# Two lone token tiles joined into a pair, batch 0's token transform with its two sums in the other order, and its first tile centred in halves

## The chip, the core and the metric

The kernel runs on one core of a Trainium2 chip. The metric is the device time of one launch in microseconds (us). A core has five engines that run side by side, each through its own list of instructions in order: PE (TensorE, matmul, with PEld for the weight loads that run ahead of it), DVE (VectorE), ACT (ScalarE), POOL (GpSimd) and SP (SyncE, which here only issues DMAs). They wait for one another by semaphores.

## The reference

For each of 8 batches there are 12 heads, 448 tokens and 64 channels per head. What is computed, cut to what matters:

```python
q_n = q / (norm(q, axis=-1) + 1e-06);  k_n likewise
attn = softmax(q_n @ k_n.T / tau)            # per head, tau = 0.1
x = (attn @ v) as (batch, 448, 768)          # heads side by side
mixed = real(fft(fft(x, axis=1), axis=2))    # tokens, then channels
u = x + mixed
un = (u - mean(u)) / sqrt(var(u) + 1e-06)    # per token
out = u + relu(un @ w_ch1) @ w_ch2           # 768 -> 3072 -> 768
```

## The kernel before

**Tiles.** The 448 tokens of a batch are held in tiles of 128. The Fourier transform is real-valued sums and differences with tables of cosines and sines, and it leaves the tokens folded: an even batch gives three whole tiles, and half a tile that shares its place with a half of the odd batch behind it; that shared tile is the odd batch's fourth. So `tiles` (L1312) lists three tiles for an even batch and four for an odd one, 28 in all.

**Stages of a batch.** `attn` (L907) makes scores (L973, L986), exponentials on ACT (L951) and the product with v (L1004, L1010). `fold` and `fsum` (L1038, L1111) sum over tokens with the token tables (matmuls L1129, L1134, L1138; their result is copied out of PSUM at L1159/L1160). `fft` (L1165) does the channel sums: the matmuls at L1181 in batch 0 and at L1188/L1191 in the others. Each batch has two of these groups, called fd0 and fd1. `uadd` adds x (L1233, L1245), and then each tile is normalised: mean (L1270/L1271), squares on ACT (L1275), logarithm and exponential (L1278, L1280), and the centring on DVE (L1282) into the buffer UN. A tile is then turned, in batch 0 by PE (L1292, copied out at L1300), in all others by a transposing DMA that SP issues (L1303), into one of the four slots of UNT.

**The two products with the weights.** `ffn` and `up` take the tiles one at a time or in pairs. The first product (L1350) takes 144 matmuls either way: 128 columns wide for a lone tile, 256 for a pair. The second (`prod`, L1494) takes 48 matmuls of 384 columns for a lone tile. For a pair it is done in seven products of quarter matrices instead of eight, with sums of the hidden quarters made on DVE (`comb`, L1593): 84 matmuls. The last three pairs do the first product in such a way too (`ups`, L1445). `units` (L1322) sets the pairs and the slots: of an even batch two tiles are a pair and one is alone. Lone are the first tile of batches 0 and 6 and the last tile of batches 2 and 4. A pair's result leaves PSUM through ACT (L1514) with an add on POOL (L1519), or through DVE (L1530).

**What sets the order.** The program is written by a planner (`schedule`, L257). Each operation has an engine, a duration from the table `TIMES`, a priority, and what it depends on; the table `SHIFT` moves single priorities. The planner walks through time and gives each engine the operation of least priority number that can start. All products with the weights hang on one another in a chain (`self.main`), so PE does them in a fixed order, with pieces of the next batch's attention set between them. Where the plan leaves PE idle, `fill` (L398) puts in six matmuls of 128 columns that compute nothing used (L1737). Up to the first product they read the identity matrix in TX, and after it W1b.

**Batch 0's tables.** ACT makes the channel tables at L645 and L647, the second being the sine table CSp. POOL makes the negated sine table from it (L659), into the tensor CSd. In batch 0 each of fd0 and fd1 is two groups of eight matmuls, first sum 0, which reads the negated table, and then sum 1, which reads CSp.

Of the kernel before, what the change touches and what calls it, by code (L numbers as in the profile page):

```python
# [13 lines left out]
DM = H * DH  # L14
# [11 lines left out]
TF = 4  # L26
ORDER = (0, 1, 2, 3, 5, 4)
# [473 lines left out]
class Kern:  # L501
# [405 lines left out]
    def attn(self, b):  # L907
# [31 lines left out]
        for pos, j in enumerate(ORDER):  # L939
# [20 lines left out]
            elif b >= 4:  # L960
                steps = [[(pos, kt) for kt in range(3)]]
            else:
                steps = [[(pos, 0), (pos, 1)], [(pos, 2), (pos + 1, 0)]] if pos % 2 == 0 else [[(pos, 1), (pos, 2)]]
# [201 lines left out]
    def fft(self, b):  # L1165
# [94 lines left out]
        for ui, ut in enumerate(order):  # L1260
# [24 lines left out]
            if b == 0 and ui == 0:  # L1285
                self.un0 = un
# [511 lines left out]
```

## Time and profile before

| what | value |
|---|---|
| runs of the kernel, median (lowest to highest of 3) | 577.16 us (577.0 to 578.32) |
| span of the profiled execution | 575.2 us |
| PE busy | 555.8 us, 97% of the span |
| DVE, ACT, POOL busy | 430.6, 385.3, 220.3 us |
| granted TensorE clock, mean | 0.999 of full speed |

The span runs from the first to the last instruction of the profiled execution; that execution's time as a run is not recorded apart from the three runs. "Busy" is the share of time in which at least one instruction of the engine ran; matmuls overlap, so sums of single durations are longer than the busy time. A bracket at the end of a timeline row is the time that the engine stood idle just before it, and who ended the wait. In the chain of waits the time given for a run of matmuls is from start to start, without the overlap.

### The profile page before, as it was taken

What the parts mean: (1) busy time and instruction counts of PE and PEld (TensorE: products, weight loads), DVE (VectorE), ACT (ScalarE), POOL (GpSimd) and SP (SyncE); (2) the same over time, 40 slices, a digit from 0 to 9 for tenths busy, and PEclk for the clock granted to TensorE, in tenths of its full rate; (3) what the DMA queues carried; (4) which work ended last, traced back from release to release, by engine and by line L of the source; (5) the groups of instructions that cost most, each with busy time, mean ns of one, the idle gap of its engine ahead of it and who ended that gap; (6) DMA issues with size and microseconds to landing.
All of it is one profiled execution on the core that took longest, in us unless ns stands there. A gap on an engine that the chain in (4) does not pass through costs nothing.

```text
span 575.2 us, 16313 instructions
## 1 busy us (share of the span) xinstructions
PE 555.8 (97%) x6766; PEld 436.2 (76%) x6766; DVE 430.6 (75%) x917; ACT 385.3 (67%) x724; POOL 220.3 (38%) x332
## 2 busy tenths in 40 slices
PE   3899999999999999999999999999999999989997
PEld 3569787676787686878788787778778787959694
DVE  8989968996669869975669669776778579986262
ACT  7898885564876885687558875577637853747270
POOL 7534414356329544612370724523270210041303
PEclk9999999999999999999999999999999999999999
DMA  9999999975459739952595429743591210023001
GB/s 188 224 233 171 166 186 130 171 152 111 111 94 103 178 76 135 142 127 62 112 121 93 102 80 147 150 84 85 89 113 29 43 57 28 2 43 72 28 28 56
DMA packets 187898, 62.20 MB, mean 108 GB/s; under 512 B 166800, under 2 KB 185616, under 8 KB 187824
## 3 DMA queue, kind: packets, MB, share of 16 engines
q1 hardware_dynamic: 129856, 38.35, 33.7%
q0 software_dynamic: 57968, 22.81, 30.9%
q8 instruction: 53, 0.87, 0.6%
q14 instruction: 21, 0.17, 0.1%
HBM read 51.90 MB, written 11.01 MB: 109 GB/s over the span
## 4 chain that ended last, share of the span: by engine, by line
PE 60%; DVE 4%; ACT 2%; issue 0%; DVEq 0%; ACTq 0%
PE PS L1494 23%; PE PS L1350 20%; PE PS L1445 6%; PE PS L1010 4%; PE PS L973 3%; DVE U L1233 1%; PE PS L1004 1%; PE PS L986 1%; ACT E L951 1%; DVE ACG L1222 1%; ACT F L1275 1%; PE PS L1134 1%; PE PS L1191 1%; DVE SM L885 1%; DVE HQ L1593 1%
## 5 line engine op out<-in xcount | busy, mean ns | idle before, releaser
L1350 PE MATMUL PS<-UNT,W1b 128*128 128x256 bf16 (+1 forms) x1872 | 186.1, 256 | 1.2 <-DMA UNT<-F 0.6
L1350 PEld LDWEIGHTS PS<-UNT,W1b 128*128 128x128 bf16 x1872 | 155.5, 98 | 20.1 <-issue 2.7
L951 ACT ACTIVATE E<-PS 128x900 bf16<-128x900 f32 (+1 forms) x192 | 148.0, 827 | 19.1 <-PE PS L973 16.6
L1494 PE MATMUL PS<-W2b,HQ 128*128 128x384 bf16 x768 | 133.1, 326 | 0.0
L896 POOL TENSOR_TENSOR QH<-STG,SM 128x256 bf16<-128x256 f32 x126 | 82.3, 679 | 91.9 <-DVE SM L702 73.3
L1494 PEld LDWEIGHTS PS<-W2b,HQ 128*128 128x128 bf16 x768 | 73.3, 98 | 46.2 <-issue 0.7
L1519 POOL TENSOR_TENSOR OUTB<-OUTB,U 128x192 f32<-128x192 f32 x66 | 43.2, 675 | 138.5 <-ACT OUTB L1514 137.3
L1366 ACT ACTIVATE HQ<-PS 128x512 bf16<-128x512 f32 x81 | 48.2, 595 | 40.0 <-PE PS L1350 39.5
L1494 PE MATMUL PS<-TX,HQ 128*128 128x384 bf16 (+2 forms) x408 | 69.7, 321 | 1.8 <-ACT MV L1278 1.6
L883 ACT ACTIVATE QH<-STG 128x384 f32<-128x384 f32 x84 | 42.7, 520 | 25.8 <-DVE SM L885 21.3
L1494 PEld LDWEIGHTS PS<-TX,HQ 128*128 128x128 bf16 x408 | 38.4, 98 | 25.7 <-ACT MV L1278 2.0
L1593 DVE TENSOR_TENSOR HQ<-HQ 128x1536 bf16<-128x1536 bf16 (+1 forms) x69 | 49.5, 721 | 9.9 <-ACT HQ L1366 7.1
L885 DVE TENSOR_REDUCE SM<-QH 128x6 f32<-128x384 f32 x84 | 44.7, 544 | 11.3 <-ACT QH L883 11.0
L1010 PE MATMUL PS<-VB,E 128*128 128x65 bf16 x1152 | 51.4, 193 | 0.0
L1366 DVE TENSOR_SCALAR HQ<-PS 128x512 bf16<-128x512 f32 x45 | 31.0, 688 | 23.8 <-PE PS L1350 23.4
L1010 PEld LDWEIGHTS PS<-VB,E 128*128 128x128 bf16 x1152 | 47.7, 97 | 1.2
L1552 POOL DMA_INDIRECT out_dram<-OUTB,IDX x21 | 23.8, 1134 | 56.9 <-DVE OUTB L1530 51.7
L1004 PE MATMUL PS<-VZ,E 128*128 128x130 bf16 x192 | 41.6, 219 | 0.5 <-ACT E L951 0.2
L973 PE MATMUL PS<-QK 64*128 64x225 bf16 (+2 forms) x864 | 39.6, 227 | 0.1
L1233 DVE SCALAR_TENSOR_TENSOR U<-ACG,X 128x768 bf16<-128x768 f32 (+4 forms) x39 | 39.1, 1015 | 0.8
L1530 DVE TENSOR_TENSOR OUTB<-PS,OUTB 128x384 f32<-128x384 f32 x33 | 18.2, 553 | 25.7 <-PE PS L1494 21.9
L1514 ACT ACTIVATE OUTB<-PS 128x384 f32<-128x384 f32 x33 | 16.1, 488 | 29.5 <-PE PS L1494 29.1
(191 smaller groups left out, 793.6 us busy)
## 6 DMA issues: line engine op xcount, KB each, us to landing
STG<-in_q_dram SPq DMA_DIRECT2D x18, 384.0 KB, 4.0
STG<-in_k_dram SPq DMA_DIRECT2D x18, 384.0 KB, 3.8
VB<-in_v_dram POOLq DMA_DIRECT2D x24, 192.0 KB, 7.1
W1b<-in_moe_w_ch_dram POOLq DMA_DIRECT2D x12, 384.0 KB, 7.7
W2b<-in_moe_w_ch_dram POOLq DMA_DIRECT2D x12, 384.0 KB, 7.2
out_dram<-OUTB SPq DMA_DIRECT2D x7, 384.0 KB, 3.4
W2b<-in_q_dram SPq DMA_DIRECT2D x2, 576.0 KB, 10.0
W2b<-in_k_dram SPq DMA_DIRECT2D x2, 576.0 KB, 10.7
```

The source lines that it names most:

```text
L885: P.add("dve", lambda v, o=SS[:, i, H // ns * x:H // ns * (x + 1)], sq=sq: v.tensor_reduce(o, sq.rearrange("p (h d) -> p h d", d=DH), AX.X ...
L896: r = v.tensor_tensor(v3(qh)[:, h:h + 4], v3(buf)[:, h:h + 4], RN[:, i, h:h + 4].unsqueeze(2).to_broadcast((128, 4, DH)), AluOp.mult)
L951: return a.activation(o, self.PS[:, bk:bk + nc_, 0:SQ2], ACTF.Exp, scale=1.0 / self.tau)
L973: i = pe.matmul(self.PS[:, bk + h, c0:c0 + n], self.KT[r, jj, kt * 128:(kt + 1) * 128], self.QT[r, jj, cols], start=True, stop=True)
L1004: r = pe.matmul(o, st(6), self.VZ[:, j, :], start=not split, stop=(split and i == 0), skip_group_check=True)
L1010: r = pe.matmul(o[:, 65 * h:65 * h + 65], st(2 * kt + h), self.VB[:, kt, 2 * j + h, :], start=(split and i == h == kt == 0), stop=((not sp ...
L1233: self.snu.append(P.add("dve", lambda v: v.scalar_tensor_tensor(two(U[o0:o0 + n, ut, :]), src, 1.0, two(X[i0:i0 + n, x, :]), AluOp.mult, A ...
L1350: r = pe.matmul(self.PS[:, bk, x * n:(x + 1) * n], self.W1b[:, j, ft * 128:(ft + 1) * 128], self.UNT[:, j, cs], start=(j == 0), stop=(j == ...
L1366: return e.activation(o, i, ACTF.Relu) if e is self.nc.scalar else e.tensor_relu(o, i)
L1494: r = pe.matmul(self.PS[:, bk, 0:n], lhs(f), rhs(f), start=(start and f == 0), stop=(stop and f == NF // 2 - 1), skip_group_check=True)
L1519: r = g.tensor_tensor(self.OUTB[:, ob, xs], self.OUTB[:, ob, xs], self.U[:, ut, xs], AluOp.add)
L1593: P.add("dve", lambda v: v.tensor_tensor(cs(o), cs(a), cs(bq), op), 0.16 + 0.3 * len(ks), -0.5, f"{nm}{ks[0]}_{b}", reads=rd, writes=[x fo ...
```

## The change

- `units` now lists the tiles of all batches in one row and takes them in pairs, but for the two named in `ONES`. The last tile of batch 4 and the first of batch 5 are a pair, then 5's second and third, then 5's fourth with the first of batch 6. So four lone tiles become two, 16 units become 15, and two pairs cross from one batch to the next.
- `HELD`: the fourth tile of batch 5 is not centred into UN, whose place the next batch's fold needs, but later, out of U into a QH buffer, behind the first product of the pair before (`unheld`).
- In batch 0, sum 1 of fd0 and fd1 comes first and sum 0 second; the negated table is tracked under a name of its own (CSm), so that only sum 0 waits for it.
- The first tile of batch 0 is centred in two halves of 384 columns, and PE turns each half by itself.
- Batch 3 issues the scores of three token blocks as one operation, as batches 4 to 7 did; before, it issued two at a time.
- Scores of a batch are ordered behind the channel sums of the batch before it.
- The planner's margins for operations that wait on DMAs are larger in four entries of `LATE`. The loads of the start are held in a written order (`QUEUES`). `SHIFT` grows from 312 names to 1751, so that operations change places in every batch.

```diff
+ONES = ((0, 0), (2, 2))
+HELD = (5, 3)
...
+QUEUES = [("ld_q1_0 ld_k0_0 ld_q0_0 ld_t0_0 ld_q2_0 ld_t1_0 ld_k1_0 ld_t2_0 ld_k2_0 ld_q0_1 ld_t0_1 ld_k0_1 ld_k1_1 ld_t1_1 ld_q1_1"),
...
-    "te0_7": {0: -660.502}, "S20": {0: 422.8735}, "c31_6": {0: 717.6321, 3: 0.5978}, "c3r1_6": {0: 473.2237}, "c41_6": {2: 825.7525},
...
-LATE = {r"W[12]_\d+": 1.5, "tmd": 2.0, r"sq\d_\d": 1.5, r"sq[KQT]\d_1": 1.5, r"ktd\d": 2.0, r"qdup\d": 2.0, ...
+LATE = {r"sq6_[2-7]": 4.0, r"W[12]_\d+": 1.5, "tmd": 2.0, r"sq\d_\d": 2.0, r"sq[KQT]\d_1": 1.5, r"ktd\d": 3.5, r"qdup\d": 4.0, ...
...
-    (0.4, 1.9), 10, "sinp", reads=["CSp"], writes=["CSd"])
+    (0.4, 1.9), 10, "sinp", reads=["CSp"], writes=["CSm"])
...
-            elif b >= 4:
+            elif b >= 3:
                 steps = [[(pos, kt) for kt in range(3)]]
...
-            for sg in (0, 1) if b == 0 else (0,):
+            for sg in (1, 0) if b == 0 else (0,):
-                                         reads=["Tt0", "Tt1", "Tt1b", "CSd"] + (["CSp"] if b == 0 and sg else []),
+                                         reads=["Tt0", "Tt1", "Tt1b", "CSd"] + ([["CSm"], ["CSp"]][sg] if b == 0 else []),
...
+            if (b, ui) == HELD:
+                self.held = (ut, rn, lp, slot, col)
+                continue
+            halves = [slice(0, 384), slice(384, DM)] if late else [slice(0, DM)]
+            for g, c in enumerate(halves):
+                un = P.add("dve", lambda v, ...: v.tensor_scalar(self.UN[:, nb_, c], U[:, ut, c], self.MV[:, ut, 0:1], ...
...
+    def unheld(self):
+        P.add("dve", lambda v: v.tensor_scalar(self.QH[:, r, :], self.U[:, ut, 0:DM], self.MV[:, ut, 0:1], self.RS[:, ut:ut + 1], AluOp.add, AluOp.mult),
+              t_dve(DM, 4) + 0.16, lp, f"un{ui}_{b}", reads=rn + [f"MV{ut}", f"RS{ut}"], writes=qn)
+        self.last_tru = P.add("sp", lambda sy, sem: sy.dma_start_transpose(self.UNT[:, :, col:col + 128], self.QH[:, r, :]).then_inc(sem, 16),
...
-            for n in (1, 2) if b in (0, self.nb - 2) else (2, 2) if b % 2 else (2, 1):
+        order = [(b, i) for b in range(self.nb) for i in range(len(self.tiles(b)))]
+        while x < len(order):
+            n = 1 if order[x] in ONES else 2
+            for y in range(n):
+                b, i = order[x + y]
+                self.slots[b][i] = 2 * (u % 2) + y
+            self.pairs.append(order[x:x + n])
...
+        for k, unit in enumerate([u for u in self.pairs if u[-1][0] == b]):
+                    self.up(b, unit, chunks, True)
+                    if unit[1][0] == HELD[0] and unit[0][0] < b:
+                        self.unheld()
```

Three places show what the planner made of it. The first is DVE in the last part of batch 6's products, where L1465 (now L1870) adds what PE left in PSUM to an earlier result, L1593 (L1999) makes the sums of hidden quarters, and L1233 (L1617) adds x for batch 7. Before:

```order
L1593 TENSOR_TENSOR HQ<-HQ 128x512
L1465 TENSOR_TENSOR HQ<-PS,E 128x384
L1233 SCALAR_TENSOR_TENSOR U,ACG<-ACG,X 97x768
L1593 TENSOR_TENSOR HQ<-HQ 128x512
L1253 COPY ACG<-ACG 1x2
L1253 COPY U<-U 1x768
L1593 TENSOR_TENSOR HQ<-HQ 128x1536
L1270 TENSOR_SCALAR MV<-ACG 128x1
L1593 TENSOR_TENSOR HQ<-HQ 128x1536
```

And in the changed kernel:

```order
L1870 TENSOR_TENSOR HQ<-PS,E 128x384 x2
L1872 TENSOR_SCALAR HQ<-HQ 128x384
L1671 TENSOR_SCALAR F<-U,MV 128x768
L1999 TENSOR_TENSOR HQ<-HQ 128x512 x2
L1999 TENSOR_TENSOR HQ<-HQ 128x1536 x2
L1606 TENSOR_TENSOR ACG<-PS,ACG 128x388
L1617 SCALAR_TENSOR_TENSOR U,ACG<-ACG,X 97x768
```

Batch 7's add of x over 97 rows, two copies and a mean stood between the last L1465 and the second large sum; they now stand behind it, and one centring (L1671) stands in front.

The second place is PE between the channel sums fd1 of batch 2 (L1188/L1191, now L1572/L1575) and the first product of that batch's first pair (L1350, now L1755). L1494 (L1899) is the second product of the unit before, L973 and L986 (L1357, L1370) are scores of batch 3, L1004 and L1010 its products with v, whose two rows come four times, right ahead of the first product. Before, behind 24 matmuls of L1494:

```order
L1494 MATMUL PS<-W2b,HQ 128x384 x8
L973 MATMUL PS<-QK 128x225 x8
L1494 MATMUL PS<-W2b,HQ 128x384 x16
L973 MATMUL PS<-QK 128x225 x8
L1494 MATMUL PS<-TX,HQ 128x384 x4
L986 MATMUL PS<-QK,KTD 128x225 x2
L1494 MATMUL PS<-TX,HQ 128x384 x8
L1004 MATMUL PS<-VZ,E 128x130
L1010 MATMUL PS<-VB,E 128x65 x6
```

And in the changed kernel, from the last two matmuls of fd1 on:

```order
L1572 MATMUL PS<-CS,E 128x96
L1575 MATMUL PS<-CS,E 128x2x96
L1899 MATMUL PS<-TX,HQ 128x384 x20
L1899 MATMUL PS<-W2b,HQ 128x384 x24
L1899 MATMUL PS<-TX,HQ 128x384 x12
L1357 MATMUL PS<-QK 128x225 x12
L2153 MATMUL PS<-W1b 128x128 x18
L1370 MATMUL PS<-QK,KTD 128x225 x2
L1755 MATMUL PS<-UNT,W1b 128x256 x24
```

Between fd1 and the first product there stood 24 + 8 + 16 + 4 + 8 = 60 matmuls of the unit before, two groups of scores, a third of two matmuls, and 28 matmuls with v. Now there are 56 of the unit before, 12 + 2 of scores and none with v, but 18 matmuls that `fill` put in (L2153). Sixteen matmuls of the unit before have gone in between fd0 and fd1, which stood side by side.

The third place is DVE behind the channel sums of batch 5 (differences L1222, now L1606; add of x L1233, now L1617; centring L1282, now L1671), whose first tile is now the partner of batch 4's last. Before, the last ten of the rows up to its centring:

```order
L1233 SCALAR_TENSOR_TENSOR U,ACG<-ACG,X 32x768
L1366 TENSOR_SCALAR HQ<-PS 128x512
L1233 SCALAR_TENSOR_TENSOR U,MV<-ACG,X 1x768
L1270 TENSOR_SCALAR MV<-ACG 128x1
L1270 TENSOR_SCALAR MV<-MV 128x1
L885 TENSOR_REDUCE SM<-QH 128x6 x2
L1366 TENSOR_SCALAR HQ<-PS 128x512
L885 TENSOR_REDUCE SM<-QH 128x6
L1366 TENSOR_SCALAR HQ<-PS 128x512
L1282 TENSOR_SCALAR F<-U,MV 128x768
```

And in the changed kernel, all rows from the differences to the centring:

```order
L1606 TENSOR_TENSOR ACG<-PS,ACG 128x388 x2
L1617 SCALAR_TENSOR_TENSOR U,ACG<-ACG,X 128x768 x2
L1606 TENSOR_TENSOR ACG<-PS,ACG 128x388
L1654 TENSOR_SCALAR MV<-ACG 128x1
L1269 TENSOR_REDUCE SM<-QH 128x6
L1606 TENSOR_TENSOR ACG<-PS,ACG 128x388
L1617 SCALAR_TENSOR_TENSOR U,ACG<-ACG,X 97x768
L1936 TENSOR_TENSOR OUTB<-PS,OUTB 128x384
L1269 TENSOR_REDUCE SM<-QH 128x6
L1671 TENSOR_SCALAR F<-U,MV 128x768
```

The first tile is centred behind 11 DVE instructions, counted from the first difference, where 27 stood before.

## Rows read from the trace of the kernel before

**Rows 1.** The page's first part: busy time, share, instructions by engine.

```profile
PE 555.8 (97%) x6766; PEld 436.2 (76%) x6766; DVE 430.6 (75%) x917; ACT 385.3 (67%) x724; POOL 220.3 (38%) x332
```

**Rows 2.** Windows: stretch, length, busy time (instructions) of each engine, clock, DMA.

```profile
0.00:48.40 48.40, 35.94 (x518) 27.82 (x518) 43.20 (x103) 41.44 (x67) 27.32 (x58) 1.00 1.31 211
48.40:571.70 523.30, 519.87 (x6250) 408.39 (x6248) 387.09 (x814) 343.83 (x658) 192.66 (x275) 1.00 0.60 99
571.70:575.20 3.50, 0.00 (x1) 0.00 (x0) 0.29 (x1) 0.00 (x0) 0.36 (x1) 0.89 0.31 112
```

**Rows 3.** Waits of PE: who, for whom, us in total, times, longest.

```profile
PE PS L1350 <- DMA UNT<-F: 0.6, 1, 0.6
```

**Rows 4.** Chain of waits: start, us from start to start, what.

```profile
236.98 4.03 PE PS L1350 x72
...
434.29 6.55 PE PS L1350 x60
```

**Rows 5.** Timeline of PE, 100 to 119: start, us, instruction, count.

```profile
103.47 13.81 PE L1494 MATMUL PS<-W2b,HQ 128*128 128x384 bf16 x84
```

**Rows 6.** Groups by form, PE: count, then busy us, mean ns, idle before.

```profile
L1350 PE MATMUL PS<-UNT,W1b 128*128 128x128 bf16 x576 | 34.1, 219 | 0.2
```

**Rows 7.** Timeline, all engines, 40.9 to 56, a choice.

```profile
40.98 1.15 ACT L759 ACTIVATE OUTB<-W2b 128x1152 f32<-128x1152 f32 x1
...
41.17 2.17 POOL L659 TENSOR_SCALAR CS<-TX 128x770 bf16<-128x770 bf16 x1 [0.31 <-ACT TX L647]
...
42.03 1.33 ACT L1159 ACTIVATE E<-PS 128x900 bf16<-128x900 f32 x2
...
42.58 1.37 PE L1737 MATMUL PS<-TX 128*128 128x128 bf16 x18 [0.17 <-DVE SM L762]
...
43.79 0.84 PE L1181 MATMUL PS<-CS,E 128*128 128x193 bf16 x8
...
46.56 0.42 DVE L1282 TENSOR_SCALAR F<-U,MV 128x768 bf16<-128x768 bf16 x1
...
47.03 0.51 PE L1292 MATMUL PS<-TX,F 128*128 128x128 bf16 x6
...
47.85 0.55 DVE L1300 CAST UNT<-PS 128x384 bf16<-128x384 f32 x1
...
48.46 7.79 PE L1350 MATMUL PS<-UNT,W1b 128*128 128x128 bf16 x126
```

**Rows 8.** Timeline of PE from fd1 of batch 2 to its first product.

```profile
182.11 4.07 PE L1494 MATMUL PS<-TX,HQ 128*128 128x384 bf16 x24
...
187.41 0.56 PE L973 MATMUL PS<-QK 64*128 64x225 bf16 x8
...
194.85 1.38 PE L1350 MATMUL PS<-UNT,W1b 128*128 128x256 bf16 x11
```

**Rows 9.** Batch 5, fd0 to first product: PE, SP and line L1303's landings.

```profile
362.16 0.21 PE L1188 MATMUL PS<-CS,E 97*128 97x96 bf16 x1
...
379.10 5.21 SPq L1303 DMA_TRANSPOSE UNT<-F  x4
...
DMA to landing us min/median/max: 2.7/2.8/5.3
...
387.59 0.78 PE L973 MATMUL PS<-QK 64*128 64x128 bf16 x24
388.30 2.79 PE L1350 MATMUL PS<-UNT,W1b 128*128 128x256 bf16 x24
```

**Rows 10.** Timeline, all engines, 503 to 507, a choice.

```profile
503.40 1.76 POOL L1519 TENSOR_TENSOR OUTB<-OUTB,U 128x192 f32<-128x192 f32 x2 [35.16 <-ACT OUTB L1514]
503.48 1.28 DVE L1593 TENSOR_TENSOR HQ<-HQ 128x1536 bf16<-128x1536 bf16 x1
...
505.22 0.96 DVE L1593 TENSOR_TENSOR HQ<-HQ 128x1536 bf16<-128x1536 bf16 x1 [0.39 <-DVE MV L1270]
...
506.32 4.06 PE L1494 MATMUL PS<-TX,HQ 128*128 128x384 bf16 x24 [1.64 <-ACT MV L1278]
```

More of the change, by code (lines that the diff above doesn't have):

```diff
@@ L977, in attn @@
                 self.last_qk = P.add("pe", fn, 0.195 * len(st_) + 0.2, pj, f"qk{j}{st_[0][1]}_{b}", reads=rd,
-                      tiles=new, acquire=new, margin=0.3, order=([self.last_qk] if self.last_qk else []) + self.pvs[-2:-1])
+                      tiles=new, acquire=new, margin=0.3, order=([self.last_qk] if self.last_qk else []) + self.pvs[-2:-1] + (self.fd_ops[-1:] if b and pos == 0 else []))
                 for tile, (ps, kt) in zip(new, st_):
@@ L1055, in fold @@
                        t_dve(512, 2) + (0.03 if b else 0.0), pj, f"f{eo}{dj}_{b}", reads=["AC0", "AC2"],
-                       writes=[f"F{eo}{dj}"] + ([f"UN{x}" for x in range(4)] if dj == 0 and eo == 0 else []),
+                       writes=[f"F{eo}{dj}"] + ([f"UN{x}{y}" for x in range(4) for y in ("", "h")] if dj == 0 and eo == 0 else []),
                        after=[self.first_f] if dj or eo else [])
@@ L1285, in fft @@
-            if b == 0 and ui == 0:
-                self.un0 = un
+            if (b, ui) == HELD:
[3 more added lines that the diff above has]
+            for g, c in enumerate(halves):
+                un = P.add("dve", lambda v, ut=ut, nb_=nb_, late=late, c=c: v.tensor_scalar(self.UN[:, nb_, c], U[:, ut, c], self.MV[:, ut, 0:1], None if late else self.RS[:, ut:ut + 1],
+                                                                                          AluOp.add, AluOp.bypass if late else AluOp.mult),
+                      t_dve(c.stop - c.start, 4) + 0.16, lp, f"un{ui}_{b}", reads=rn + [f"MV{ut}"] + [f"RS{ut}"] * (not late), writes=[f"UN{nb_}" + "h" * g] + [f"UN{nb_}h"] * (not late))
@@ L1287, in fft @@
             if b == 0:
                 tile = Tile("G")
-                def fn(pe, tile=tile, nb_=nb_):
-                    for j in range(NJ):
-                        r = pe.matmul(self.PS[:, self.bank(tile) + j // 3, 128 * (j % 3):128 * (j % 3) + 128],
-                                      self.UN[:, nb_, 128 * j:128 * j + 128], self.ID, start=True, stop=True)
-                    return r
-                P.add("pe", fn, 0.4, lp, f"tn{ui}_{b}", reads=[f"UN{nb_}", "ID"], tiles=(tile,), acquire=tile)
+                tns = []
@@ new lines, in fft, with fn @@
+                for g in range(2) if late else (None,):
+                    def fn(pe, tile=tile, nb_=nb_, g=g):
+                        for j in range(NJ) if g is None else range(3 * g, 3 * g + 3):
+                            r = pe.matmul(self.PS[:, self.bank(tile) + j // 3, 128 * (j % 3):128 * (j % 3) + 128],
+                                          self.UN[:, nb_, 128 * j:128 * j + 128], self.ID, start=True, stop=True)
+                        return r
+                    tns.append(P.add("pe", fn, 0.2 if late else 0.4, lp, f"tn{ui}_{b}", reads=[f"UN{nb_}" + "h" * (g == 1), "ID"] + [f"UN{nb_}h"] * (g is None), tiles=(tile,), acquire=None if g else tile))
@@ L1300, in ev @@
                         return e.activation(o, i, ACTF.Copy) if e is self.nc.scalar else e.tensor_copy(o, i)
-                    self.evac(ev, 384, lp, f"eu{ui}{g}_{b}", writes=[f"uT{slot}" + "xy"[g]], after=(tile.users[0],), tiles=(tile,))
+                    self.evac(ev, 384, lp, f"eu{ui}{g}_{b}", writes=[f"uT{slot}" + "xy"[g]], after=(tns[g if late else 0],), tiles=(tile,))
                 continue
@@ L1322, in units @@
     def units(self):
[L1324 to L1330 removed]
+        self.slots = [[0] * len(self.tiles(b)) for b in range(self.nb)]
+        order = [(b, i) for b in range(self.nb) for i in range(len(self.tiles(b)))]
+        u = x = 0
+        self.pairs = []
+        while x < len(order):
[4 more added lines that the diff above has]
+            self.pairs.append(order[x:x + n])
+            u, x = u + 1, x + n
     def hid(self, q, ft0, n=1):
@@ L1520, in plus @@
                 return r
-            self.P.add("pool", plus, 1.07, -1, f"{nm}p_{b}", reads=[on] + self.unames(b, ut), writes=[on])
+            self.P.add("pool", plus, 1.07, -1, f"{nm}p_{b}", reads=[on] + self.unames(bt, ut), writes=[on])
             return op
@@ L1531, in fin @@
         on = f"OUT{ob}" + "b" * c + "z" * (c0 > 0)
-        return self.P.add("dve", fn, t_dve(c1 - c0), -1, f"{nm}_{b}", reads=([on] if src == "out" else self.unames(b, ut)) + [f"RS{ut}"] * late, writes=[on],
+        return self.P.add("dve", fn, t_dve(c1 - c0), -1, f"{nm}_{b}", reads=([on] if src == "out" else self.unames(bt, ut)) + [f"RS{ut}"] * late, writes=[on],
                           after=(op,), tiles=(tile,))
@@ L1729, in build @@
             op.prio = round(op.prio + SHIFT.get(op.name, {}).get(k, 0), 4)
+        named = {op.name: op for op in self.P.ops if op.dma is not None}
+        for q in QUEUES:
+            q = [named[n] for n in q.split()]
+            for x, y in zip(q, q[1:]):
+                y.order += (x,)
         self.est = self.P.schedule()
```

88 lines of the change are left out of this document (45 added, 43 removed), and 499 rows, old and new, of tables (SHIFT, TIMES).

## The prediction, made before the changed kernel ran

> **What bounds the kernel now.** I read the engine summary first, then windows over the launch, then PE's waits, and only then the places that the change touches. In the summary PE is busy for 97% of the span, DVE for 75% [rows 1]. The windows split this into three parts [rows 2]. Up to 48.4 us, before the first product with the weights, PE works for only 35.94 us, so there a chain through other engines sets the time. From 48.4 to 571.7 us PE is busy for 519.87 of 523.30 us, which leaves 3.43 us idle in all. The last 3.5 us have no matmul. So in the long middle part PE's own work is the path: a microsecond of matmuls that goes is a microsecond off the end, as long as no new wait takes its place, and all waits together can give back at most 3.43 us. Two waits stand out: 1.64 us in the middle of batch 6's products [rows 10], and 0.6 us on a turned tile, once [rows 3].
>
> The sum is made against the profiled span of 575.2 us. The median of the runs is 577.16 us, 1.96 us more, which lies outside the span; I add it unchanged. A measurement of this kernel can tell about 0.3% from no change, 1.7 us, so "the same" is 575.4 to 578.9.
>
> **A. Two pairs in place of four lone tiles.** In the chain a lone tile's 72 matmuls of the first product take 4.03 us and a pair's 60 take 6.55 [rows 4]; both kinds have 144, so 8.06 and 15.72 us. The second product of a pair, 84 matmuls of 384 columns, takes 13.81 us with the end of the last one, 13.65 from start to start, or 0.1625 each [rows 5]; a lone tile's 48 take 7.80. Two lone tiles cost 2 x (8.06 + 7.80) = 31.72 us, a pair 15.72 + 13.65 = 29.37: 2.35 us less. That is for each two lone tiles joined; what does the whole change join? Four lone tiles become two, but in the order (4, 2), (5, 0), ... the pairs in between only shift by one, so one pair is gained: minus 2.35 us. The other bound is the group by form, where 576 lone matmuls are busy for 34.1 us, 8.5 for each of the four tiles [rows 6]; with it the saving is 2 x (8.5 + 7.8) - 29.37 = 3.3. I take 2.35, since the chain counts from start to start, which is what PE's path adds up.
>
> The row gives 4.03 / 72 = 56 ns for a matmul of 128 columns and 6.55 / 60 = 109 for one of 256. The Trainium skill (TensorE: Matmul & The Clock Gate, Back-to-back issue gap) puts a sustained stream of loads and matmuls of 128 columns at about 81 ns each. By that a lone first product would take 11.7 us and the pair save some 7 us more. The trace disagrees with the page, whose isolated gap of about 56 ns is what the rows show, and the sum goes by the rows.
>
> The pair adds seven sums of hidden quarters and a few results on DVE, and six adds on POOL. DVE is idle for a quarter of the span [rows 1] and these lie beside 29 us of matmuls, so I put them at nothing. Without that cover each would cost its length. What speaks against it: the large sum on DVE takes 0.96 us alone and 1.28 beside POOL's add [rows 10], 0.32 more for a collision; six more adds, all on DVE's path, would cost 6 x 0.32 = 1.9 us. The Trainium skill (GPSIMD Engine Reference, Specifications) says why this may be: POOL's SBUF interfaces are shared with VectorE, and an instruction of the latter with two SBUF inputs contends. The rows agree.
>
> **B. The start.** The chain that releases batch 0's channel sums ended three times nearly together: POOL's negated table at 41.17 + 2.17 = 43.34, ACT's second copy of token sums at 42.03 + 1.33 = 43.36, and PE's filling matmuls, which ran until fd0 began at 43.79 [rows 7]. So waiting no longer for the negated table doesn't bring much: ACT's copy is late next, and ACT now sets a square of 1.15 us (L759) [rows 7] between the two copies. I take 0.2 us, with bounds of 0 and 0.45 (43.79 - 43.34). From the centring (46.56) to the first product (48.46) lie centring 0.42, six turning matmuls 0.51 and the copy out 0.55. In halves, PE can turn the first half and the copy can start while DVE centres the second: two halves of some 0.25 to 0.3 for one of 0.42, but half of the 0.51 is hidden, and the first copy comes earlier. I take 0.3, bounds 0 and 0.45. Together minus 0.5, bounds minus 0.9 and 0.
>
> **C. The first product of batch 2.** Before, fd1 ended at 182.11 and the first product began at 194.85 [rows 8], 12.7 us later: the length of the chain (differences, add of x, normalising, turning) in that plan, and all of it was filled with matmuls. In the changed plan (the second place of the order) 56 matmuls of 0.1625 = 9.1 us stand between, 14 scores at 0.07 (0.56 / 8) [rows 8] = 1.0, together 10.1, and then filling matmuls, which are put in where the plan itself leaves PE idle. If the chain still takes 12.7, PE loses 2.6 us; if it has become shorter, because sixteen matmuls now let fd0's part run 2.6 us ahead of fd1, it loses nothing. Bounds 0 and 2.7; I take the middle, plus 1.3.
>
> **D. The wait in batch 6.** PE stands still for 1.64 us before a quarter product, and the sum that it needs is the second large one, which DVE began at 505.22 behind small sums for batch 7, the first large one stretched to 1.28 [rows 10]. In the changed order (the first place) the add of x, two copies and the mean stand behind the two large sums, and one centring of 0.42 [rows 7] in front. Between the two large sums lay 505.22 - 503.48 - 1.28 = 0.46 us, most of it a wait for the mean; the add of x in front of the first I put at about the 0.96 of a large sum, an estimate, since both read two tensors of some hundred rows. So the second sum comes 0.46 + 0.96 - 0.42 = 1.0 us earlier: minus 1.0, bounds minus 1.64 and, if POOL's adds collide with the sums once or twice more at 0.32, plus 0.5.
>
> **E. The rest.** Batch 3's scores in threes instead of twos, the larger margins, the written order of the loads and the shifts of single priorities take no PE work away. They lie beside a PE that idles for under 1%. I put them at nothing, with 0.3 us either way; by the order PE's filling matmuls go from 156 to 162, and six more of 1.37 / 18 [rows 7] are 0.5 us in places where PE has nothing else to do.
>
> Sum: -2.35 - 0.5 + 1.3 - 1.0 = -2.55. Span 572.65, time **574.6 us**. All bounds to one side give 571.0 and 578.3.
>
> **The rivals.**
> First, the gain is eaten: the chain at C holds the full 2.6 us, D gives nothing, and the crossing pair waits a little too, as its second tile comes from the next batch. Then -2.35 - 0.3 + 2.6 + 0 = about 0, 577.1 us. For it: every wait of before was just covered, with one tile's landing already late by 0.6 [rows 3]; against it: the planner had freedom over a whole batch to set the order.
>
> Second, slower: the pair (4, 2) with (5, 0) must wait for batch 5's first tile. Before, that batch's channel sums began at 362.16, the tile was sent to be turned at 379.10, and landed 2.8 us later [rows 9]: a chain of 19.7 us, while the first product began only at 388.30, so it had room. Now between those channel sums and the pair's first product stand 60 matmuls of the second product (9.75), 48 scores (24 in 0.71, so 1.4) [rows 9] and the channel sums themselves, 1.1 (from the eight of batch 0 in 0.84) [rows 7]: with a handover some 12.4 us. With a chain as long as before PE would stall for 7.3 us: 574.6 + 7.3 = 581.9. It makes the kernel slower from a chain of 12.4 + 2.55 + 1.73 = 16.7 us on. Against it: the first tile is centred behind 11 DVE instructions where 27 stood (the third place of the order), which leaves out most of the 19.7.
>
> Third, more gain: the waits at C and D go altogether, and the saving at A is the larger one: 577.16 - 2.35 - 0.5 - 1.64 - 0.4 = about 572.3 us.
>
> **How the numbers follow.** My forecast has 0.60, with a range of its own of 572.9 to 576.7; about 0.08 of it lies above 575.4. The first rival has 0.14, nearly all within 0.3%; the slower one 0.14, nearly all above 578.9; the larger gain 0.12. Faster: 0.52 + 0.12 = 0.64; same: 0.08 + 0.13 = 0.21; slower: 0.15. The range goes from 572.0 to 578.3, which takes in the forecast, the first rival and most of the third; the slower rival and the ends are left out.
>
> **What the profile of the changed kernel would show.** For A, 1440 matmuls of 256 columns and 288 of 128 in the first product, at 109 and 56 ns. For B, the first product at about 47.9 us, where it was at 48.46. For C, a wait of PE of 0 to 2.7 us, or filling matmuls, before the first product of batch 2; for D, no wait over 0.7 us in batch 6's products. For the slower rival, PE waiting for a turned tile before the pair of batches 4 and 5. I am wrong if PE's idle time after 48 us is well over 4 us, or if a busy PE takes longer for the same matmuls.

## The result, and the profile after

The changed kernel takes 579.23 us (median of 20 runs, 578.17 to 580.43) where the kernel before takes 578.39 (20 runs, 577.00 to 579.56). The ratio is 1.0014, with a 95% interval of 1.0007 to 1.0020: not faster, but a little slower, by 0.8 us. Forecast were 574.6 us and a gain of 2.55. The median of before is also 1.2 us above the 577.16 that the forecast started from: those three runs were on the quick side.

The page of the changed kernel begins, in the columns of [rows 1]:

```profile
PE 555.4 (96%) x6616; PEld 434.8 (75%) x6616; DVE 441.1 (76%) x921; ACT 385.4 (67%) x728; POOL 229.6 (40%) x338
```

There are 150 matmuls fewer, yet PE is busy for only 0.4 us less. DVE has four instructions more and is busy for 10.5 us more. The windows, cut like [rows 2] at the first product and 3.5 us before the end (behind that cut the changed kernel still has eight matmuls), say where the time went:

```profile
0.00:48.82 48.82, 36.66 (x506) 28.65 (x506) 43.43 (x102) 41.27 (x66) 27.79 (x58) 1.00 1.28 208
48.82:574.30 525.48, 518.30 (x6106) 405.89 (x6107) 397.11 (x819) 344.16 (x663) 200.98 (x280) 1.00 0.63 98
574.30:577.80 3.50, 0.42 (x8) 0.24 (x5) 0.57 (x2) 0.00 (x0) 0.78 (x1) 1.00 0.31 112
```

In the long middle part PE works 1.57 us less than before (518.30 for 519.87), but it is idle for 525.48 - 518.30 = 7.18 us where it was 3.43. The first part is 0.42 us longer. Together -1.57 + 3.75 + 0.42 = +2.60 us, which is the difference of the spans (577.8 and 575.2).

The work that goes is what the pairing takes away. Groups by form of the two products, after (count, then busy us, mean ns):

```profile
L1755 PE MATMUL PS<-UNT,W1b 128*128 128x256 bf16 x1440 | 168.6, 273 | 0.8 <-ACT KTD L1227 0.4 <-DVE HQ L1771 0.4
L1755 PE MATMUL PS<-UNT,W1b 128*128 128x128 bf16 x288 | 17.0, 219 | 0.4 <-ACT UNT L1688 0.3 <-DVE TX L1771 0.2
L1899 PE MATMUL PS<-W2b,HQ 128*128 128x384 bf16 x720 | 124.1, 326 | 0.0
L1899 PE MATMUL PS<-TX,HQ 128*128 128x384 bf16 x420 | 74.1, 326 | 1.3 <-DVE OUTB L1936 1.3
```

and the same groups before, of which one is in [rows 6]:

```profile
L1350 PE MATMUL PS<-UNT,W1b 128*128 128x256 bf16 x1296 | 152.0, 273 | 0.9 <-DMA UNT<-F 0.6 <-DVE QK L799 0.3
L1494 PE MATMUL PS<-W2b,HQ 128*128 128x384 bf16 x768 | 133.1, 326 | 0.0
L1494 PE MATMUL PS<-TX,HQ 128*128 128x384 bf16 x384 | 67.5, 326 | 1.8 <-ACT MV L1278 1.6
```

Sums: 383.8 us after, 386.7 before with the 34.1 of [rows 6]. By this count the pair saved 2.9 us, and 1.4 us of it went into filling matmuls (below). What is new is the idle time. PE's list of waits of the changed kernel (total, times, longest) has these behind the start's, where [rows 3] had 0.6 us for a turned tile:

```profile
PE PS L1518 <- DVE F L1482: 2.3, 3, 1.0
PE PS L1899 <- DVE OUTB L1936: 1.3, 1, 1.3
...
PE PS L1522 <- DVE F L1482: 1.0, 1, 1.0
PE PS L2153 <- DVE U L1617: 0.9, 1, 0.9
```

L1518 and L1522 are the sums over tokens: four times, in batches 3 to 6, PE stands still ahead of them (0.96, 0.41, 0.90 and 0.99 us, some 3.3 in all) for DVE's last sum of the fold. Before, PE never waited there. The 1.3 us of L1899 lie ahead of batch 2's first product: DVE stood behind a late add on POOL, and PE behind DVE's result, which frees its bank in PSUM:

```profile
190.82 0.56 DVE L1936 TENSOR_TENSOR OUTB<-PS,OUTB 128x384 f32<-128x384 f32 x1 [2.32 <-POOL OUTB L1925]
...
191.43 2.13 PE L1899 MATMUL PS<-TX,HQ 128*128 128x384 bf16 x12 [1.34 <-DVE OUTB L1936]
```

The timeline of batch 5 shows what DVE does meanwhile (all engines, a choice of rows):

```profile
356.07 4.49 POOL L1280 TENSOR_TENSOR QH<-STG,SM 128x256 bf16<-128x256 f32 x6 [2.22 <-DVE SM L1086]
356.97 1.75 DVE L1478 TENSOR_TENSOR F<-ACG 128x772 bf16<-128x772 bf16 x2
358.75 1.35 DVE L1482 TENSOR_TENSOR F<-F 128x388 bf16<-128x388 bf16 x2
360.15 1.00 PE L1518 MATMUL PS<-CS,F 128*128 128x113 bf16 x16 [0.90 <-DVE F L1482]
```

POOL scales q and k of the next batch (L1280) while DVE does the last four sums of the fold, and each of these takes half as long again or more. In the kernel before, the first of these two scalings began 5 us behind that fold:

```profile
359.73 1.75 POOL L896 TENSOR_TENSOR QH<-STG,SM 128x256 bf16<-128x256 f32 x3 [2.42 <-DVE SM L702]
```

Over the whole launch, DVE's sums of the folds by form, before (L1094, L1098) and after (L1478, L1482; mean ns behind the busy us):

```profile
L1094 DVE TENSOR_TENSOR F<-ACG 128x772 bf16<-128x772 bf16 x8 | 4.2, 558 | 0.0
L1098 DVE TENSOR_TENSOR F<-F 128x388 bf16<-128x388 bf16 x8 | 2.6, 362 | 0.1
```

```profile
L1478 DVE TENSOR_TENSOR F<-ACG 128x772 bf16<-128x772 bf16 x8 | 6.3, 821 | 0.2 <-ACT ACG L1475 0.2
L1482 DVE TENSOR_TENSOR F<-F 128x388 bf16<-128x388 bf16 x8 | 4.0, 533 | 0.1
```

The same instructions, 47% longer. DVE's sums with one input in PSUM are as long as before, 551 ns for 553, with POOL beside them or not. The Trainium skill (GPSIMD Engine Reference, Specifications) has POOL and VectorE share their SBUF interfaces, with contention for DVE instructions that read two SBUF inputs or run in a 2-port mode; for the sums of two SBUF inputs these rows agree. They are not the only ones: DVE's scaling in the fold (L1475), which reads one SBUF tensor, took 0.65 us beside POOL in batch 5 and 0.42 without it in batch 4; in which mode it ran the trace doesn't tell.

The kernel before had such meetings as well. In batch 3's fold POOL's add lay over the last sums, of which the first took 1.20 us for 0.35:

```profile
229.37 1.12 POOL L1519 TENSOR_TENSOR OUTB<-OUTB,U 128x192 f32<-128x192 f32 x2
229.52 1.20 DVE L1098 TENSOR_TENSOR F<-ACG 128x388 bf16<-128x388 bf16 x1
```

PE didn't wait there: the last of these sums was done 0.58 us before the token sum.

### The profile page after: what moved, and what is told of

It reads as the page before. It is cut to its first block, busy times and chain, and to the rows that moved or that the text cites. A ratio compares the mean times of both kernels' runs of the same rounds, so it can differ in the third digit from the quotient of the medians.

```text
span 577.8 us, 16053 instructions
## 1 busy us (share of the span) xinstructions
PE 555.4 (96%) x6616; PEld 434.8 (75%) x6616; DVE 441.1 (76%) x921; ACT 385.4 (67%) x728; POOL 229.6 (40%) x338
## 4 chain that ended last, share of the span: by engine, by line
PE 82%; DVE 9%; ACT 3%; POOL 2%; issue 2%; DMA 1%; SPq 1%; POOLq 0%; DVEq 0%; ACTq 0%
PE PS L1755 28%; PE PS L1899 28%; PE PS L1850 7%; PE PS L1394 5%; PE PS L1357 5%; PE PS L1388 2%; ACT E L1335 2%; PE PS L1370 1%; DVE HQ L1999 1%; DMA TX<-in_k_dram 1%; DVE U L1617 1%; POOL QH L1280 1%; SPq L1136 1%; DVE F L1438 1%; DVE ACG L1431 1%
## 5 line engine op out<-in xcount | busy, mean ns | idle before, releaser
L1755 PE MATMUL PS<-UNT,W1b 128*128 128x256 bf16 (+1 forms) x1728 | 185.6, 264 | 1.2 <-ACT KTD L1227 0.4
L1755 PEld LDWEIGHTS PS<-UNT,W1b 128*128 128x128 bf16 x1728 | 153.4, 98 | 20.8 <-issue 1.8
L1280 POOL TENSOR_TENSOR QH<-STG,SM 128x256 bf16<-128x256 f32 x126 | 87.2, 718 | 95.5 <-DVE SM L1086 45.7
L1899 PE MATMUL PS<-W2b,HQ 128*128 128x384 bf16 x720 | 124.1, 326 | 0.0
L1899 PEld LDWEIGHTS PS<-W2b,HQ 128*128 128x128 bf16 x720 | 68.8, 98 | 43.7 <-ACT OUTB L1920 0.5
L1925 POOL TENSOR_TENSOR OUTB<-OUTB,U 128x192 f32<-128x192 f32 x72 | 50.4, 720 | 120.2 <-ACT OUTB L1920 118.7
L1899 PE MATMUL PS<-TX,HQ 128*128 128x384 bf16 (+2 forms) x444 | 76.2, 322 | 1.3 <-DVE OUTB L1936 1.3
L1899 PEld LDWEIGHTS PS<-TX,HQ 128*128 128x128 bf16 x444 | 41.6, 98 | 27.9 <-DVE OUTB L1936 2.1
L1999 DVE TENSOR_TENSOR HQ<-HQ 128x1536 bf16<-128x1536 bf16 (+1 forms) x73 | 54.3, 748 | 8.0 <-ACT HQ L1771 4.8
L1269 DVE TENSOR_REDUCE SM<-QH 128x6 f32<-128x384 f32 x84 | 45.4, 547 | 19.4 <-ACT QH L1267 18.0
L1958 POOL DMA_INDIRECT out_dram<-OUTB,IDX x21 | 21.8, 1036 | 69.2 <-DVE OUTB L1936 29.1
L1617 DVE SCALAR_TENSOR_TENSOR U<-ACG,X 128x768 bf16<-128x768 f32 (+4 forms) x39 | 39.1, 1010 | 0.8
L1357 PE MATMUL PS<-QK 64*128 64x225 bf16 (+2 forms) x864 | 39.3, 228 | 0.1
L1936 DVE TENSOR_TENSOR OUTB<-PS,OUTB 128x384 f32<-128x384 f32 x36 | 19.8, 551 | 24.0 <-PE PS L1899 17.6
```

What stands on the lines that cost most here:

```text
L1269: P.add("dve", lambda v, o=SS[:, i, H // ns * x:H // ns * (x + 1)], sq=sq: v.tensor_reduce(o, sq.rearrange("p (h d) -> p h d", d=DH), AX.X ...
L1280: r = v.tensor_tensor(v3(qh)[:, h:h + 4], v3(buf)[:, h:h + 4], RN[:, i, h:h + 4].unsqueeze(2).to_broadcast((128, 4, DH)), AluOp.mult)
L1357: i = pe.matmul(self.PS[:, bk + h, c0:c0 + n], self.KT[r, jj, kt * 128:(kt + 1) * 128], self.QT[r, jj, cols], start=True, stop=True)
L1617: self.snu.append(P.add("dve", lambda v: v.scalar_tensor_tensor(two(U[o0:o0 + n, ut, :]), src, 1.0, two(X[i0:i0 + n, x, :]), AluOp.mult, A ...
L1755: r = pe.matmul(self.PS[:, bk, x * n:(x + 1) * n], self.W1b[:, j, ft * 128:(ft + 1) * 128], self.UNT[:, j, cs], start=(j == 0), stop=(j == ...
L1899: r = pe.matmul(self.PS[:, bk, 0:n], lhs(f), rhs(f), start=(start and f == 0), stop=(stop and f == NF // 2 - 1), skip_group_check=True)
```

## The experiments

"Changed" below is the changed kernel (579.2 us); each kernel ran beside the kernel before on one chip, and ratios are to that. Before's own median on these chips lay between 578.2 and 578.6 us. Edits change the order that the planner has written, add a wait to it, or shrink or leave out work; nothing is planned anew. In the names of the expectations the last number is the batch: h0_2 is the first product of batch 2, m10 to m72 are quarter products of the second product, fd the channel sums, te the copies of the token sums out of PSUM, sc the scalings of q and k on POOL, names with p_ the adds on POOL, fin results that DVE adds, S and s sums for the quarter products.

**The kernel before once more.** No edit.

> The kernel before once more, unchanged, for a second trace. My theory, that the first trace was taken in an execution with quick loads at the start: the first token sum (fs0 of batch 0) begins about 0.8 us later than the 37.95 us of the first trace, near the changed kernel's 38.72, and from there on the two traces of before agree to 0.3 us. The rival, that the written order of the loads made the changed kernel's start later: the token sum begins at 37.9 again.

Measured: 578.13 us. First row: the first token sum in the first trace of before; then, of the second trace, that sum and the first product:

```profile
37.95 0.77 PE L1129 MATMUL PS<-CS,F 128*128 128x225 bf16 x6
```

```profile
39.06 0.77 PE L1129 MATMUL PS<-CS,F 128*128 128x225 bf16 x6
...
49.56 1.62 PE L1350 MATMUL PS<-UNT,W1b 128*128 128x128 bf16 x26
```

The start came 1.1 us later, the rest is the same: 10.50 us to the first product (10.51 before), and the middle part again lasts 523.30 us. So the first trace of before had a quick start, and the written order of the loads isn't needed to explain the changed kernel's 38.72. Over all traces of this study the first token sum begins between 37.6 and 39.8 us; spans of single executions are compared only behind it.

**Seven POOL operations held back until the fold is done ("hold").**

```diff
+HOLD = {"fm0p_2": ("e1_3", 0), "fv0p_3": ("g1_4", 1), "fm0p_3": ("e1_4", 0), "sc5_6": ("e1_5", 0), "sc6_6": ("e1_5", 0), ...}
+        for late, (n, k) in HOLD.items():
+            for op in (x for x in self.P.ops if x.name == late):
+                op.deps.add(kth(n, k))
```

> The changed kernel with every engine's order unchanged, but seven POOL operations that ran beside the folds of batches 3 to 6 wait until that fold's last sums (for one, its second difference) are done. My theory, that POOL beside the fold stretches DVE's sums and so makes PE wait ahead of the token sums: DVE's sums of 772 columns (L1478) fall from a mean of 0.82 us to about 0.56, PE's four waits of 0.96, 0.41, 0.90 and 0.99 us before token sums of batches 3 to 6 go, and the time falls by 2.5 to 3.3 us against the changed kernel (to about 576.3 where it shows 579.2, some 2 us under before). The rival, that the order of the fold among other DVE work sets these waits and the collisions are hidden: the waits stay within 0.3 us and the time doesn't move. A second rival: the held scalings of q and k come too late for the next scores, and the time doesn't fall although the four waits go.

Measured: 580.19 us, ratio 1.0032 (1.0017 to 1.0047). All four waits ahead of token sums are gone, and the sums of 772 columns take 0.559 us. But the time didn't fall, where 2.5 to 3.3 us were expected. DVE now stands behind the POOL work that comes late, and PE behind DVE (two DVE rows and one of PE, in the held kernel):

```profile
362.61 0.56 DVE L1938 TENSOR_TENSOR OUTB<-PS,OUTB 128x384 f32<-128x384 f32 x1 [3.53 <-POOL OUTB L1927]
...
427.27 0.96 DVE L1794 TENSOR_TENSOR STG<-W1b 128x1536 bf16<-128x1536 bf16 x1 [4.06 <-POOL QH L1282]
...
429.29 0.22 PE L1574 MATMUL PS<-CS,E 97*128 97x96 bf16 x1 [1.79 <-DVE E L1546]
```

The mechanism of my theory held, its time didn't: the second rival was right in the main, with the lateness paid on DVE's queue and not at the scores.

**One scaling moved behind two adds on POOL ("swap"), and both edits together ("both").**

```diff
+        line = self.P.order["pool"]
+        late = [x for x in line if x.name == "sc5_3"]
+        line.remove(late[0])
+        line.insert([x.name for x in line].index("fm2p_1") + 1, late[0])
```

> The changed kernel with one move: on POOL, the scaling sc5_3 (three instructions, 3.0 us) behind the adds fv2p_1 and fm2p_1 instead of ahead of them. My theory, that DVE stood 2.3 us behind a late POOL add, which kept PE's bank occupied (wait of 1.34 us before m42_1) and held up the centring of batch 2's tiles (0.93 us and 18 filling matmuls before h0_2): both waits go, and the time falls by about 2.2 us. The rival, that batch 2's chain of normalising and turning tiles sets the first product there whatever POOL does: the 1.34 us go, but the wait before h0_2 grows by as much, and the time doesn't move.

> Both edits together, the seven waits and the moved scaling. If the two places are separate losses of the changed kernel, their gains add: 4.5 to 5.5 us under the changed kernel, about 574, some 4 us under before, near the time forecast. If PE's idle time only moves on (to later waits for POOL's held work), the time stays within 1 us of the changed kernel.

Measured: 584.78 us, ratio 1.0115 (1.0094 to 1.0135), and 585.30, 1.0134 (1.0105 to 1.0163). The 1.34 us went, but two larger waits came (PE, moved scaling alone):

```profile
194.90 0.76 PE L1357 MATMUL PS<-QK 64*128 64x225 bf16 x12 [2.26 <-DMA QK<-QH]
...
201.00 1.22 PE L1755 MATMUL PS<-UNT,W1b 128*128 128x256 bf16 x5 [3.96 <-DMA UNT<-F]
```

The scaled tile is turned by a DMA that SP issues in order. It came late for the scores, and behind it on SP's queue stood the three turns of batch 2's tiles, which began at 194.38 where the changed kernel has them at 191.79. I had not counted SP's queue. Neither theory nor rival had this, and the gains of the two edits don't add in "both" either.

**The same POOL work shrunk instead of held ("light", "light2").** The code for the scalings:

```diff
-                    for h in range(0, H, 4):
+                    for h, n in ((0, 1),) if f"sc{i}_{b}" in LIGHT else ((0, 4), (4, 4), (8, 4)):
```

> The changed kernel with its order and its waits, but the seven POOL operations beside the folds of batches 3 to 6 shrunk in place: the four scalings do one head of twelve, the three adds 48 of 384 columns (the rest of these scalings and adds is left out, and the squares of those four tiles are written in bf16 in half the space). So nothing is held back and nothing comes later. My theory, that POOL running beside the fold is what stretches it and makes PE wait: the four waits of 0.96, 0.41, 0.90 and 0.99 us go, nothing takes their place, and the time falls by about 3 us against the changed kernel, to about 576. The rival, that the order of this plan makes PE wait at one place or another whatever POOL does: less than 1 us is gained.

> As the run before it, and two more scalings shrunk, sc4_3 and sc5_3, which in the changed kernel keep POOL busy until 188.0 us, ahead of the two adds that DVE and then PE wait for. My theory, that POOL's queue makes the waits before m42_1 (1.34 us) and h0_2 (0.93): both go, and the time falls by another 2 us, to about 574. The rival, that batch 2's chain of normalising and turning sets h0_2: the 1.34 us go, but h0_2 starts no earlier relative to the end of its channel sums, and less than 0.7 us is gained.

Measured: "light" 575.51 us, ratio 0.9948 (0.9935 to 0.9961), 3.7 us under the changed kernel; the four waits are gone and nothing over 0.35 us took their place. Windows around the end of batch 6's fold, changed kernel first, then "light":

```profile
421.00:426.60 5.60, 4.22 (x39) 3.31 (x37) 5.57 (x9) 2.14 (x4) 5.06 (x7) 1.00 1.30 106
```

```profile
417.00:422.60 5.60, 5.60 (x55) 5.03 (x54) 5.41 (x13) 3.27 (x6) 2.67 (x4) 1.00 1.59 110
```

PE is idle for 1.38 of 5.60 us beside a POOL that is busy for 5.06, and not at all beside one that is busy for 2.67. "light2" 575.12, 0.9953 (0.9937 to 0.9969): between these two the medians can't tell. In its trace the 1.34 us are gone and the wait before batch 2's first product is 0.69 for 0.93 us, some 1.6 us in all of the 2 expected; from the end of that batch's channel sums to its first product it is 12.0 us for 13.8, so that product does start earlier, against the rival, though the medians don't show it.

The shrunk squares don't speed anything up by themselves: in "a_light" below, where all are shrunk, DVE's 84 sums over them take 547 ns each and ACT's writes 521, as in the changed kernel.

**Only batches 3 and 4 held ("hold34"), and "hold" with two moves ("best").**

```diff
+        move("pool", "fa0p_4", "sc6_6")
+        move("dve", "S10", "S20")
```

> Of the seven added waits only the three on POOL's adds beside the folds of batches 3 and 4. From the run with all seven: up to the fold of batch 5 it had gained 1.2 us against the changed kernel, and it lost more behind batches 5 and 6, where DVE stood behind POOL's late work (3.5 and 4.1 us idle). My theory, that what is lost comes from the four held scalings alone: 1.0 to 1.3 us under the changed kernel. The rival, that any POOL work held back costs later what it gave: within 0.5 us of the changed kernel.

> All seven waits, and two moves that take DVE out from behind POOL's late work: on POOL the add fa0p_4 ahead of the scaling sc6_6, and on DVE the sum S10 (which overwrites what the scaling reads, and is not needed before the last products) behind the copy te0_6 and the sum s11_5. My theory, that the seven waits failed for these two blocked places only: PE's waits of 0.45 and 0.59 us before m50_4 and m70_4 and of 1.79 us before fd1_6 go, and the time is 3 to 4.5 us under the run with the seven waits, near 576, some 2 us under before. The rival, that a plan this full gives PE a new wait for each one removed: within 1.5 us of the changed kernel.

Measured: "hold34" 578.25 us, ratio 0.9998 (0.9989 to 1.0006), 1.0 under the changed kernel, as my theory had it, and level with before. "best" 579.58, 1.0015 (1.0006 to 1.0024), where some 576 was expected: the three waits went, and new ones of 0.70 (batch 5's channel sums, for ACT) and 1.03 us came:

```profile
433.76 1.47 PE L1901 MATMUL PS<-W2b,HQ 128*128 128x384 bf16 x8 [1.03 <-ACT HQ L1773]
```

The rival was right there.

**Two adds exchanged ("add1st"), no filling matmuls ("nofill"), and the mild edits together ("final").**

```diff
+        move("pool", "fm2p_1", "fv2p_1")
...
-        self.P.fill(first, self.est - 20.0, self.id_op, warm(self.W1b[:, 0, 0:128]), 0.75)
```

> The changed kernel with two POOL adds exchanged, fm2p_1 ahead of fv2p_1; nothing is held back, and the scaling sc5_3 stays ahead of both. DVE's next result (fin31_1, which frees PE's bank) needs only fm2p_1; who needs fv2p_1 comes 2.4 us later. My theory, that POOL's queue makes the 1.34 us before m42_1: that wait falls under 0.3 us, DVE's centrings come about 1.4 us earlier with it, and the time falls by 1.3 to 1.6 us against the changed kernel. The rival, that PE waits at h0_2 instead: the wait before h0_2 grows, and less than 0.5 us is gained.

> The changed kernel without the 24 filling matmuls that stand behind the first product (6 in batch 1's start, 18 before h0_2). Each of these groups waits for a DVE operation, and the 18 begin 0.93 us late and take 1.4 us. My theory, that they stand where PE would wait for batch 2's turned tile anyway: the first product there starts at most 0.5 us earlier, and the time falls by 0 to 0.5 us. The rival, that the filling itself is what PE waits for: 1 to 2.3 us are gained. A third, that without them the granted clock falls behind the idle stretch: the clock of that stretch is under 1.00 and the time rises.

> The three edits that hold nothing up for others in one kernel: the three waits on POOL's adds beside the folds of batches 3 and 4, fm2p_1 ahead of fv2p_1, and no filling matmuls behind the first product. If they are separate losses, 1.0 + 1.4 + 0.3 = 2.7 us under the changed kernel, about 576.5 where it shows 579.2, and some 2 us (0.3%) under before. If PE's waits only move on, within 1 us of the changed kernel.

Measured: "add1st" 580.25 us, ratio 1.0026 (1.0016 to 1.0036). The 1.34 us are gone, but the wait before batch 2's first product grew from 0.93 to 1.23, and further on PE waited at places that the edit doesn't touch (0.64, 0.46, 1.00 us, the last for a turned tile). From the end of the channel sums to that product it is 12.7 us, 1.1 less than in the changed kernel, so part of the gain is there and is lost later. Waits at the same places, of 0 to 1.2 us, are in several other traces, so I can't tell how much of this is the edit's; my theory failed on the time. "nofill" 579.76, 1.0016 (1.0002 to 1.0030): no gain in the time. In the trace PE waits in the fillers' stead, with a granted clock of 1.00 in that stretch, and begins the first product 0.3 us sooner behind the channel sums (13.5 us for 13.8):

```profile
195.26 0.37 PE L1370 MATMUL PS<-QK,KTD 128*128 128x225 bf16 x2 [1.84 <-DMA UNT<-F]
```

So the fillers stood in a wait for the turned tile. "final" 578.11, 0.9999 (0.9990 to 1.0008): 1.1 us under the changed kernel where 2.7 were expected, and level with before. In its trace PE waits 2.15 us just before batch 2's first product. No version here that computes all of the output beats the kernel before.

**POOL's work shrunk everywhere, in both kernels ("b_light", "a_light").** The shrinking of "light" for all scalings from batch 2 on and all adds.

> The kernel before with all POOL scalings from batch 2 on and all POOL adds of results shrunk in place (one head of twelve, 48 of 384 columns; the rest of them is left out, and the squares are written in bf16 in half the space). Partner of the next run. In the kernel before, PE never waits ahead of token sums; only the 1.64 us in batch 6's products contain a sum stretched by POOL (1.28 for 0.96 us). My theory, that before had its POOL work where it disturbs nobody: 0.3 to 1.2 us under before. The rival, that POOL beside DVE costs this kernel as much as the changed one: 2.5 us or more.

> The changed kernel with the same work shrunk. My theory, that the step at which the forecast failed is POOL's work beside DVE, at all places of the new order: the time falls by 5 us or more against the changed kernel, to 574 or below, and lies 2.5 to 4 us under the kernel before shrunk in the same way, which is the gain forecast. The rival, that the new order is itself tighter and loses whatever POOL does: less than 1 us under the kernel before shrunk in the same way.

Measured: before shrunk 576.62 us, ratio 0.9969 (0.9959 to 0.9980), 1.6 under before, a little more than I expected; changed kernel shrunk 572.34, 0.9899 (0.9881 to 0.9918), 6.9 under the changed kernel. Their middle parts, the shrunk kernel before first:

```profile
50.25:572.10 521.85, 519.05 (x6250) 408.68 (x6248) 375.02 (x815) 344.42 (x659) 94.60 (x157) 1.00 0.62 99
```

```profile
47.90:565.60 517.70, 516.38 (x6104) 406.66 (x6105) 378.44 (x819) 343.86 (x663) 96.99 (x161) 1.00 0.67 100
```

With POOL's work out of the way the changed kernel is 4.3 us the faster of the two by the medians, 4.15 by the middle parts, and PE's idle time there falls from 7.18 to 1.32 us. In the kernel before it falls from 3.43 to 2.80. So the new order is not slow of itself: of PE's idle time some 6 us hang on POOL's work, and before 0.6. DVE's busy time in these parts shows that POOL got in its way in both kernels: with the shrunk work it falls from 387.1 to 375.0 us before and from 397.1 to 378.4 after, and the instructions that got shorter are mostly those with two SBUF inputs. So before lost 12 us of DVE's time in the same way, but mostly in places where PE did not have to wait.

## Why the prediction was wrong

By its own steps, from the two traces:

| step | forecast, us | measured, us |
|---|---|---|
| A, two pairs for four lone tiles | -2.35 | -2.9 |
| B, batch 0's sums in the other order: first token sum to fd0 | -0.2 | -0.37 (5.47 for 5.84) |
| B, centring in halves: centring to first product | -0.3 | -0.03 (1.87 for 1.90) |
| C, from fd1 to batch 2's first product | +1.3 | +3.6 (1.34 and 0.93 idle, 1.36 of fillers) |
| D, the wait in batch 6 | -1.0 | -1.64 (gone) |
| the 0.6 us wait of [rows 3] | none | -0.6 (gone) |
| E, "the rest" | 0, +/- 0.3 | +3.7 (3.3 before token sums, 0.39 in batch 5) |
| start up to the first token sum | none | +0.8 (37.95 and 38.72, differs by run) |
| sum | -2.55 | +2.6 |

A and D were right. A's -2.9 is counted by busy groups, as the forecast's other bound of -3.3 was. D's wait went altogether, and the pair of batches 4 and 5 had no wait ahead of it: the slower rival didn't come. B's sum came out by luck, since its two parts missed in opposite ways. The halves brought next to nothing, because ACT's copy of the second half out of PSUM came last, behind its squares of the same tile (0.92 us from 47.39 on):

```profile
44.19 0.34 PE L1565 MATMUL PS<-TX,E 128*128 128x193 bf16 x2
...
46.96 0.55 DVE L1671 TENSOR_SCALAR F<-U,MV 128x384 bf16<-128x384 bf16 x2
...
48.31 0.47 ACT L1688 ACTIVATE UNT<-PS 128x384 bf16<-128x384 f32 x1
...
48.83 1.35 PE L1755 MATMUL PS<-UNT,W1b 128*128 128x128 bf16 x21 [0.25 <-ACT UNT L1688]
```

The step that failed first is E: "They lie beside a PE that idles for under 1%. I put them at nothing, with 0.3 us either way." Measured are 3.3 us ahead of four token sums and 0.39 in batch 5's first product. C was too small as well: its bound of 2.7 takes the stretch from fd1 to the first product to be at most as long as before, 12.7 us, but it became 13.8, with the 1.34 us behind POOL's late add in it. From the matmul behind fd1 (first row) to the first product (second):

```profile
182.77 2.44 PE L1899 MATMUL PS<-TX,HQ 128*128 128x384 bf16 x14
...
196.57 2.78 PE L1755 MATMUL PS<-UNT,W1b 128*128 128x256 bf16 x24
```

The prediction's own sign came: PE's idle time after 48 us is 7.18 us, well over 4.

A PE that never idles says nothing of the room in the chains that feed it. In the kernel before, DVE's last sum of the fold was done only 0.6 to 0.9 us ahead of the token sum in batches 3, 4 and 6, and 2.2 in batch 5. Two things used that up. The new order itself leaves less room: with POOL's work shrunk, the last sum is done 1.36, 0.83, 2.24 and 0.89 us ahead in the kernel before ("b_light", batches 3 to 6), and 0.05, 0.61, 0.63 and 0.68 in the new order ("light"). And beside POOL the folds of all four batches are stretched, by 1.2 to 2.2 us; before, only those of batches 3 and 6 were, by some 0.8 and 0.6.

[Rows 10] had shown the mechanism, 1.28 us for 0.96 beside POOL, and the prediction priced it, but at the wrong place: for the six adds that the pair brings, hidden by DVE's idle quarter. What collided were scalings and adds that were there before, and that the new plan put beside the folds. The order of one engine can't show that. It takes the orders of POOL and DVE side by side: whatever POOL does between the fold's first and last sum.

How much of it is POOL? "light" says 3.7 us by the medians for the four folds alone (3.0 in the two traces, from the first product to the last matmul), and the two shrunk kernels say that, without most of POOL's work, a gain of 4.3 us is there, more than the 2.55 forecast. That POOL's work ate the gain is shown. At the four folds it is the collision itself: "hold" left that work whole and only moved it, and the sums went back to 0.56 us and the waits were gone. At C 1.34 us are POOL's lateness, a wait that went in "add1st" and "light2". The shrunk kernels take away both, so how their 6.9 us divide stays open. So does which part of the new plan (`SHIFT`, the margins, the order of loads and scores) took the room and moved POOL's work: no run has the pair without the new plan.

Holding POOL back did not bring the gain: POOL's work is somebody's input, and late it cost as much as beside the fold or more ("hold", "best", "swap"). The mildest edits ("hold34", "final") gave 1 us and came level with before.

The base was off too: 577.16 was a median of three quick runs, and 20 give 578.39. With the right base the forecast would have been 575.8, still 3.4 us under what came. The first rival, the gain eaten by waits and a time within 0.3%, is what happened, by the ratio, and its stall at C came, larger than its 2.6 us. But D did give back its wait, the crossing pair didn't wait, and the waits at the folds it didn't have.

## What to carry to other kernels

Where one engine is busy for 97%, count the slack of each chain that feeds it, not its idle time: a plan that packs work closer spends that slack, and then every stretch of an instruction shows in the time. When an order changes, lay POOL's list beside DVE's, and look for DVE sums with two SBUF inputs that now run beside POOL's: how many there are says less than how much room is behind each. To see whether such a meeting is the cause, shrink the suspected work in place: holding it back also tests everybody who waits for it.

## What the runs showed of the hardware

- DVE's sum of two SBUF tensors of 772 bf16 columns takes 0.56 us alone and 0.85 to 0.97 beside POOL's TENSOR_TENSOR (batches 5 and 6 of the changed kernel); that of 388 takes 0.36 and 0.65 to 0.77. POOL slows down too: three scaling instructions take 1.75 us alone ("hold") and 2.28 to 2.31 beside batch 6's fold. DVE's sum of 384 columns with one input in PSUM takes 0.55 us in both kernels, and so does its TENSOR_REDUCE of 384 columns (L1269), beside POOL or not.
- The start, up to the first token sum, took 37.6 to 39.5 us in traces with the changed kernel's start, and 38.0 to 39.8 in those with that of before, so the spread is more than the whole effect of this change; behind it the two traces of before agree to 0.01 us in their middle part.
